# An attention and MLP kernel: a second output product made of seven small ones, with q's exps and row sums moved

## The chip, the cores and the metric

The kernel runs on one core of a Trainium2 chip. The metric is the device time of one execution in microseconds. The runs of the kernel before gave 255.63, 255.73 and 256.14 us; the median, 255.73, is the time before. The engines are named as in the profile: PE (matrix multiplications), PEld (PE's weight loads), DVE (VectorE), ACT (ScalarE), POOL (GpSimd) and SP (SyncE, here only an issuer of DMAs).

## The reference

Linear attention over 8 batches and 8 heads, 576 tokens of 64 values, and then a two-layer network with an exact GELU on the 4608 rows of 512 values:

```python
q_s = exp(q - max(q, axis=-1));  q_s = q_s / (sum(q_s, axis=-1) + 1e-09)
k_s = exp(k - max(k, axis=2));   k_s = k_s / (sum(k_s, axis=2) + 1e-09)
kv  = einsum('bhsd,bhse->bhde', k_s, v)
x   = einsum('bhsd,bhde->bhse', q_s, kv)      # (8, 8, 576, 64)
x   = x.transpose(0, 2, 1, 3).reshape(4608, 512)
h   = x @ w_in                                 # (4608, 2048)
g   = 0.5 * h * (1 + erf(h / sqrt(2)))
out = g @ w_out                                # (4608, 512)
```

All inputs and the output are float32. The matrix products run in bfloat16 with float32 sums. The maxima are left out in the kernel, since they cancel in the quotients.

## The kernel before

**Chunks.** The rows are worked in nine chunks. Chunk c, 0 to 7, holds the first 512 tokens of batch c; chunk 8 holds the last 64 tokens of all batches. For each chunk there is a phase for the hidden layer (x times w_in, then GELU into g) and one for the output (g times w_out). Chunks 0 and 1 are written apart; chunks 2 to 8 are the loop at the end (L1186): `h_waves` (L478), then `y_phase` (L770), or `y_last` for chunk 8. The order is the order of the program text: each engine works through its own instructions in that order and waits where it needs another engine's result. SP's DMAs go the same way, in one queue, but SP has little else to wait for and so runs far ahead of the text.

**Products by Strassen's scheme in Winograd's form.** Both layers multiply 2 x 2 blocks with seven block products in place of eight. In the output phase the left operand is g, its halves by tokens and by hidden index, and sums of them (tiles s12 and s5, made by `s_parts`, L409, on DVE at the end of the hidden phase); the right operand is w_out's blocks and sums of them, made once. `y_operands` (L682) lists the seven pairs. A product has 256 tokens, 1024 hidden values and 256 output columns: 2 groups of tokens times 8 steps of 128, 16 matmuls of 256 columns. c11, c12, c21 and c22 are the four blocks of the chunk's output, in SBUF.

**Product 3 in seven parts.** From chunk 3 on, product 3 is itself made in this way (class `Two`, from L695): seven small products of four matmuls with 128 columns. Their left operands are quarters of s12's half and four sums of them; POOL makes these sums each chunk (`Two.sums`, L712; four instructions of 128x512 in bfloat16). The sums of the weights were made once (`Two.weights`, L703). Two PSUM banks take the results, "yf" (X, four small blocks) and "yd" (D, one block that collects). `Two.add` (L748) adds them on DVE into c12: the letters a, b and c are adds from D, e and d are adds from X.

**The output phase in order.** PE: product 1, product 5, product 6, small product 1, product 2 (bank "yc"), product 7, small products 6, 5, 2, 4, 3 and 7; then, in `next_x` (L1167), the x matmuls of the next chunk and the kv matmuls of the chunk after that, and product 4. DVE: the copy of c22 (L800), the add for c12, D's adds, `q_sums`, the add of product 2 into c11, the add of product 7 into c22, the copy of one x tile, sums of x for the next hidden phase. ACT: the copy of c11 (L797), the table of Exp, `exp_q` (four instructions) and `exp_k` (one) of the batch two chunks on, the table of GELU, three x tiles, and the copy of c21 after product 4. POOL: a touch of one column that waits for DVE's last sum (`touch_s`, L1163), product 3's four sums, and the eight instructions of `q_scale_parts` (L287). SP: the loads of q, k and v for three chunks on, q's transpose by DMA (`xbar_step`, L345), two stores.

**The hidden phase in order.** PE runs the seven products in waves over eight PSUM banks (`h_waves`, L478), the first two of the four quarters of a half, then the last two. DVE makes sums of x (`x_sums`, L460), adds the e sums (`e_sum`, L526) and r sums (`r_sum`, L529) that give the GELU's inputs, and at the end the sums of g. ACT copies partial results and runs the GELUs. POOL casts v of the batch two chunks on (`cast_v_all`, L192), after a touch of one of the x sums.

**Buffers.** q's, k's inputs have two buffers each, v's input from batch 4 on has one; the other v buffer holds product 3's sums. `roles` (L470) says which PSUM bank has which use, and turns once per chunk.

Of the kernel before, what the change touches and what calls it, by code (L numbers as in the profile page):

```python
# [8 lines left out]
FP32 = mybir.dt.float32  # L9
# [7 lines left out]
def kernel(  # L17
# [87 lines left out]
        for i in range(parts):  # L105
            nc.sync.dma_start(out=f[:, i * n:(i + 1) * n, :], in_=src[:, i * n:(i + 1) * n, :])

    def v_buf(b):

        i = b % 2 if b < 4 else 0  # L110
        return f32in.tile([128, HP, NS * D], FP32, tag=f"vf{i}", name="f", bufs=1)

    def load_pair(b, name, t, parts=1):
        f = v_buf(b) if name == "v" else f32in.tile([128, HP, NS * D], FP32, tag=name + "f")
        st[b][name + "f"] = f
        src = t[b].rearrange("h (p n) d -> (h p) (n d)", n=NS).rearrange("(x q) f -> q x f", q=128)
        n = HP // parts
        for i in range(parts):
            h0 = i * n
            if b == 0 and name == "k" and i == 0:  # L120

                nc.scalar.dma_start(out=f[:, 0, :], in_=src[:, 0, :])
                h0 = 1
            nc.sync.dma_start(out=f[:, h0:(i + 1) * n, :], in_=src[:, h0:(i + 1) * n, :])

    def load_k1(i):

        if i == 0:
            st[1]["kf"] = f32in.tile([128, HP, NS * D], FP32, tag="kf", name="f")
        src = k[1].rearrange("h (p n) d -> (h p) (n d)", n=NS).rearrange("(x q) f -> q x f", q=128)  # L130
        nc.sync.dma_start(out=st[1]["kf"][:, 2 * i:2 * i + 2, :], in_=src[:, 2 * i:2 * i + 2, :])

    def load_v1(i):

        if i == 0:
            st[1]["vf"] = v_buf(1)
        src = v[1].rearrange("h (p n) d -> (h p) (n d)", n=NS)
        nc.sync.dma_start(out=st[1]["vf"][:, i, :], in_=src[i * 128:(i + 1) * 128, :])

    def load(b):  # L140
        load_main(b, "q", q)
        load_pair(b, "k", k)
        load_pair(b, "v", v)

    def load_qrest():
        f = f32in.tile([128, 2048], FP32, tag="qf")
# [325 lines left out]
    def turn_roles():  # L472
# [2 lines left out]
        roles.update(bb=r["bb"], ba=r["kv1"], x0=r["x3"], x1=r["kv0"], x2=r["x0"], x3=r["ba"],  # L475
                     kv0=r["x1"], kv1=r["x2"])

    def h_waves(c, mid):  # L478


# [60 lines left out]
        if mid:  # L541
            seed(1)
            mm(1, 2, 3)
            mm(2, 0, 1)
            gelu("C", 0, 1)
            mm(5, 0, 1)
            p5_copy(0, scopy)
            p5_copy(1, scopy)
            x_sums(c, (3, 4))
            seed(2, vcopy)  # L550
            seed(3, vcopy)
            mm(6, 0, 1)
# [24 lines left out]
            gelu("r", 2, 3)  # L577
            mm(3, 2, 3)
            mm(4, 2, 3)
        else:  # L580
            mm(5, 0, 1)
            seed(1)
            p5_copy(0, scopy)
            p5_copy(1, scopy)
            mm(6, 0, 1)
            x_sums(c, (3,))
            e_sum(0)
            e_sum(1)
            x_sums(c, (4,))
            if c + 2 < B:  # L590
                nc.gpsimd.tensor_copy(out=scr[:, 2:3], in_=t4[:, 0, 0:1])
                cast_v_all(c + 2)
            mm(2, 0, 1)
            gelu("C", 0, 1)
            mm(7, 0, 1)
            r_sum(0)
            r_sum(1)
            mm(3, 0, 1)
            for q in (2, 3):
                mm(5, q)  # L600
                mm(1, q)
            mm(4, 0, 1)
            gelu("r", 0)
            gelu("B", 0, 1)
            gelu("r", 1)
            seed(2)
            seed(3)
            gelu("A", 0, 1)
            p5_copy(2, vcopy)
            p5_copy(3, vcopy)  # L610
            s_parts(c, 0, 4, (1,))
            mm(6, 2, 3)
            e_sum(2)
            e_sum(3)
            s_parts(c, 0, 4, (2,))
            mm(2, 2, 3)
            gelu("C", 2, 3)
            mm(7, 2, 3)
            r_sum(2)
            r_sum(3)  # L620
            gelu("r", 2, 3)
            mm(3, 2, 3)
            mm(4, 2, 3)
# [7 lines left out]
        else:  # L631
            s_parts(c, 0, 4, (3, 4))
            s_parts(c, 4, 4, (1, 2, 3, 4))
        turn_roles()
        if mid:
            roles.update(ba=roles["x2"], x2=roles["ba"])
# [57 lines left out]
    class Two:  # L694
# [8 lines left out]
        def weights(self):  # L703
            (b11, b12), (b21, b22) = self.halves(self.raw_w(), slice(0, 4))
            t1, t2, t3, t4 = (self.w[:, i] for i in range(4))
            for o, i0, i1 in ((t1, b12, b11), (t2, b22, t1), (t3, b22, b12), (t4, b21, t2)):
                tt(o, i0, i1, ALU.subtract, eng=nc.gpsimd)

        def raw_w(self):
            return wo_bf[:, DN, HN:DM]  # L710

        def sums(self, c):  # L712

            (a11, a21), (a12, a22) = self.halves(y_operands(c)[0][self.m], slice(0, 4))
            s1, s2, s3, s4 = (self.s[:, i] for i in range(4))
            tt(s1, a21, a22, eng=nc.gpsimd)
            for o, i0, i1 in ((s2, s1, a11), (s4, a12, s2), (s3, a11, a21)):
                tt(o, i0, i1, ALU.subtract, eng=nc.gpsimd)

        def begin(self, c, X, D):  # L720
            self.A, self.W = y_operands(c)[0][self.m], self.raw_w()
            self.X, self.D = X, D
            self.begun = set()

        def mm(self, *sets):

# [32 lines left out]
                }[i]  # L759
                tt(t, t, x)  # L760

    def two_begin():

        t = f32in.tile([128, 9, 512], BF16, tag="vf1", name="two", bufs=1)
        two[3] = Two(3, *(t[:, i:i + 4].rearrange("p x (i n) -> p x i n", i=4) for i in (0, 4)))
        two[3].weights()

    two = {}

    def y_phase(c, ins):  # L770
# [21 lines left out]
            for fn in ins.get(i, []):  # L792
                fn()

        t3 = two[3] if c > 2 else None
        mm(1, pa, True)
        (nc.vector.tensor_copy if c == 1 else nc.scalar.copy)(out=c11, in_=halves(pa))  # L797
        after(1)
# [1 line left out]
        nc.vector.tensor_copy(out=c22, in_=halves(pb))  # L800
        after(5)
        mm(6, pa, False)
        if t3:
            tt(c12, halves(pa), c22)
            t3.begin(c, bank(at["yb"], "yf"), bank(roles["kv1"], "yd"))
            t3.mm(1)
            t3.add("a", c12)
        else:
            tt(halves(pb), halves(pa), c22)
        after(6)  # L810
        mm(2, pc, True)
        tt(c11, c11, halves(pc))
        after(2)
        mm(7, pa, False)
        if t3:
            t3.mm(6, 5, 2, 4, 3)
            t3.add("b", c12)
            t3.mm(7)
            if c + 2 < B:
                t3.add("c", c12)  # L820
        tt(c22, halves(pa), c22)
        if t3 and c + 2 >= B:
            t3.add("c", c12)
        after(7)
        if not t3:
            mm(3, pb, False)
            nc.scalar.copy(out=c12, in_=halves(pb))
            y_store(c, 0, ysb[0])
            after(3)
        else:  # L830
            ins[3][0](lambda: t3.add("ed", c12))
            y_store(c, 0, ysb[0])
        mm(4, pa, False)
        nc.scalar.copy(out=c21, in_=halves(pa))
        y_store(c, 1, ysb[1])
        after(4)

    def y_last(c):

# [293 lines left out]
    for m in (3, 2, 4, 1):  # L1133
# [11 lines left out]

    y_phase(1, {
        1: [sums[3], lambda: norm_q(2, 0, 2)],
        6: [lambda: norm_q(2, 1, 2, nc.vector), lambda: cast_v_all(3), two_begin, lambda: xbar_step(2), lambda: exp_q(3)],
        2: [lambda: kv_step(2), lambda: exp_k(3)],
        7: [lambda: q_sums(3)],  # L1150
        3: [lambda: table(AF.Gelu)],
        4: [lambda: load(4), lambda: x_all(2, (3, 4, 1, 5)),
            lambda: kv_step(3, lambda: x_sums(2, (1,))), lambda: x_sums(2, (2,))],
    })

    def q_late():


        nc.gpsimd.tensor_copy(out=scr[:, 2:3], in_=quad["r"][:, 0, 0, 0:1])
        q_scale(3, nc.gpsimd)  # L1160
        xbar_step(3)

    def touch_s():  # L1163

# [18 lines left out]
        if fn:  # L1183
            fn()

    for c in range(2, B + 1):  # L1186
        nb = c + 2
        h_waves(c, q_late if c == 2 else None)
        yi = {}
        if nb <= B:  # L1190
            yi[1] = [lambda: exp_q(nb)]
            yi[6] = [lambda: q_sums(nb), lambda: q_scale_parts(nb)]
            yi[7] = [lambda: table(AF.Gelu)]
        if nb + 1 < B:
            yi[6].append(lambda: load(nb + 1))
        elif nb + 1 == B:
            yi[6].append(load_qrest)
        if nb < B:
            yi[5] = [lambda: exp_k(nb), touch_s]
            if c == 2:  # L1200
                yi[5].append(lambda: cast_v_all(nb))
        if 2 < c < B:
            yi.setdefault(5, []).append(lambda: two[3].sums(c))
        if c < B:
            yi[3] = [lambda *fn: next_x(c, nb, *fn)]
            y_phase(c, yi)
        else:
            y_last(c)


# [28 lines left out]
```

## Time and profile before

| what | value |
|---|---|
| median of the runs | 255.73 us |
| profiled execution | 255.67 us |
| its span, first to last instruction | 253.9 us |
| granted TensorE clock, mean | 0.999 |
| busy time in 98.6 to 124.3 (about chunk 3's period): PE, DVE, ACT, POOL | 25.70, 20.34, 21.50, 11.68 us of 25.70 |
| the same in 124.3 to 150.0 | 25.70, 21.01, 21.85, 12.29 us of 25.70 |
| the same in 200.7 to 225.7 (about chunk 7's) | 25.00, 18.64, 14.08, 6.02 us of 25.00 |

A line of the timeline gives the start in microseconds from the span's start, the length, the engine, the line of the program, the operation, what it writes and reads with shapes, how many instructions were merged into it, and in brackets the idle time of the engine before it and what ended it. Matmuls are pipelined: the distance between two starts is what a group costs PE, and the length of the last one reaches some 0.16 us into the next. PEld is PE's weight loads; they run ahead of the matmuls by about 0.1 us.

### The profile page before, as it was taken

What the parts mean: (1) busy time and instruction counts of PE and PEld (TensorE: products, weight loads), DVE (VectorE), ACT (ScalarE), POOL (GpSimd) and SP (SyncE); (2) the same over time, 40 slices, a digit from 0 to 9 for tenths busy, and PEclk for the clock granted to TensorE, in tenths of its full rate; (3) what the DMA queues carried; (4) which work ended last, traced back from release to release, by engine and by line L of the source; (5) the groups of instructions that cost most, each with busy time, mean ns of one, the idle gap of its engine ahead of it and who ended that gap; (6) DMA issues with size and microseconds to landing.
All of it is one profiled execution on the core that took longest, in us unless ns stands there. A gap on an engine that the chain in (4) does not pass through costs nothing.

```text
span 253.9 us, 6709 instructions
## 1 busy us (share of the span) xinstructions
PE 247.0 (97%) x2738; PEld 195.9 (77%) x2738; DVE 195.9 (77%) x352; ACT 191.4 (75%) x334; POOL 82.6 (33%) x112
## 2 busy tenths in 40 slices
PE   7799999999999999999999999999999999999994
PEld 3444445448888888889888988898888888998883
DVE  1878699877987986898789877987788889478932
ACT  4785988699887986899788968896887687068810
POOL 1530023000945065408640774077007700700000
PEclk9999999999999999999999999999999999999999
DMA  7999999994289998980199109400700070012033
GB/s 235 400 397 427 399 407 399 398 413 172 56 260 371 239 375 259 314 332 1 34 293 403 63 20 296 102 0 6 250 0 3 0 250 0 3 67 101 1 83 85
DMA packets 43166, 50.23 MB, mean 198 GB/s; under 512 B 20224, under 2 KB 30464, under 8 KB 42880
## 3 DMA queue, kind: packets, MB, share of 16 engines
q1 hardware_dynamic: 42416, 49.13, 56.3%
q10 hardware_dynamic: 720, 0.69, 1.0%
q8 instruction: 21, 0.34, 0.5%
q14 instruction: 9, 0.07, 0.1%
HBM read 36.70 MB, written 9.44 MB: 182 GB/s over the span
## 4 chain that ended last, share of the span: by engine, by line
PE 93%; DMA 4%; ACT 0%; ACTq 0%; issue 0%; DVE 0%; POOL 0%
PE ya L785 20%; PE qa L512 19%; PE ps L401 11%; PE qb L512 10%; PE yb L785 6%; PE ps L658 6%; PE qc L512 5%; PE yc L785 5%; PE ya L857 2%; DMA touch<-in_moe_w_in_dram 2%; DMA f<-in_v_dram 2%; PE kv L225 2%; PE yf L743 2%; PE ps L367 2%; PE yb L857 1%; PE yd L743 1%
## 5 line engine op out<-in xcount | busy, mean ns | idle before, releaser
L512 PEld LDWEIGHTS <-quad_s 128*128 128x128 bf16 x448 | 43.8, 98 | 5.3
L785 PEld LDWEIGHTS <-g 128*128 128x128 bf16 x448 | 43.0, 98 | 5.9 <-issue 0.4
L512 PEld LDWEIGHTS <-wi_bf 128*128 128x128 bf16 x336 | 32.9, 98 | 4.0 <-issue 0.2
L512 PE MATMUL qa<-quad_t,quad_s 128*128 128x256 bf16 x224 | 29.4, 272 | 0.0
L401 PE MATMUL ps<-xT,wi_bf 128*128 128x512 bf16 x128 | 28.1, 379 | 0.0
L785 PEld LDWEIGHTS <-s 128*128 128x128 bf16 x256 | 25.0, 98 | 2.9
L785 PE MATMUL ya<-w,g 128*128 128x256 bf16 x224 | 26.8, 273 | 0.0
L444 DVE TENSOR_TENSOR qb<-qa,r 128x512 f32<-128x512 f32 x28 | 18.2, 694 | 11.0 <-ACT r L524 4.5
L292 POOL TENSOR_TENSOR e<-e,recq 128x256 bf16<-128x256 bf16 x40 | 24.7, 655 | 4.0 <-issue 2.1
L283 POOL TENSOR_TENSOR e<-e,recq 128x1024 bf16<-128x1024 bf16 (+1 forms) x4 | 9.3, 2332 | 48.5 <-DVE recq L278 41.8
L394 ACT CAST xT<-ps 128x512 bf16<-128x512 f32 x23 | 12.3, 593 | 16.7 <-PE ps L372 8.4
L277 DVE TENSOR_REDUCE qsum<-e 128x16 f32<-128x1024 bf16 (+1 forms) x12 | 20.9, 1741 | 4.7 <-ACT e L173 4.6
L401 PEld LDWEIGHTS <-wi_bf 128*128 128x128 bf16 x128 | 12.4, 98 | 15.1 <-issue 0.5
L407 ACT ACTIVATE g<-ps 128x512 bf16<-128x512 f32 x32 | 17.6, 602 | 6.1 <-PE ps L401 5.8
L536 ACT ACTIVATE g<-r 128x512 bf16<-128x512 f32 x28 | 17.3, 631 | 6.2 <-DVE r L444 6.2
L173 ACT ACTIVATE e<-f 128x512 bf16<-128x512 f32 (+1 forms) x42 | 20.5, 556 | 2.0 <-DMA f<-in_q_dram 1.8
L444 POOL TENSOR_TENSOR two<-s 128x512 bf16<-128x512 bf16 x10 | 11.6, 1156 | 29.8 <-DVE s L444 29.8
L536 ACT ACTIVATE g<-qc 128x512 bf16<-128x512 f32 x28 | 15.2, 594 | 6.4 <-PE qc L512 6.4
L444 DVE TENSOR_TENSOR r<-qa,r 128x512 f32<-128x512 f32 x28 | 18.0, 683 | 0.8 <-PE qa L512 0.7
L190 POOL CAST v_aug<-f 128x576 bf16<-128x576 f32 x25 | 17.3, 732 | 2.7 <-DMA f<-in_v_dram 2.6
L178 ACT ACTIVATE ek<-f 128x2304 bf16<-128x2304 f32 (+1 forms) x10 | 17.2, 1726 | 0.5 <-DMA f<-in_k_dram 0.5
L785 PE MATMUL yb<-wo_bf,s 128*128 128x256 bf16 x144 | 17.2, 273 | 0.0
(114 smaller groups left out, 492.8 us busy)
## 6 DMA issues: line engine op xcount, KB each, us to landing
out_dram<-y_sb SPq DMA_DIRECT2D x16, 512.0 KB, 3.8
f<-in_k_dram SPq DMA_DIRECT2D x6, 1152.0 KB, 10.1
f<-in_v_dram SPq DMA_DIRECT2D x6, 1152.0 KB, 11.1
f<-in_q_dram SPq DMA_DIRECT2D x6, 1024.0 KB, 7.6
w<-in_moe_w_in_dram SPq DMA_DIRECT2D x6, 512.0 KB, 8.9
f<-in_v_dram SPq DMA_DIRECT2D x8, 288.0 KB, 6.2
f<-in_q_dram SPq DMA_DIRECT2D x4, 512.0 KB, 9.0
w<-in_moe_w_out_dram SPq DMA_DIRECT2D x2, 1024.0 KB, 11.9
```

What stands on the lines that cost most here:

```text
L173: nc.scalar.activation(out=dst[:, i], in_=src[:, u], func=AF.Exp)
L178: nc.scalar.activation(out=ek[b % 2][:, i:i + n], in_=st[b]["kf"][:, i:i + n].rearrange("p x (n d) -> p x n d", n=NS), func=AF.Exp,)
L190: eng.tensor_copy(out=o, in_=i)
L277: nc.vector.reduce_sum(out=qsum, in_=st[b]["eq"][:, :, i * w:(i + 1) * w, :], axis=AX.X)
L292: nc.gpsimd.tensor_tensor(out=e, in0=e, op=ALU.mult, in1=st[b]["recq"][:, j, i:i + 4].unsqueeze(2).to_broadcast([128, 4, D]),)
L401: nc.tensor.matmul(ps, wi_bf[:, dm, t * 128:(t + 1) * 128], st[c]["xT"][:, dm, :], start=(dm == 0), stop=(dm == NDM - 1),)
L407: nc.scalar.activation(out=st[c]["g"][:, t, :], in_=ps, func=AF.Gelu)
L444: eng.tensor_tensor(out=out, in0=in0, in1=in1, op=op)
L512: nc.tensor.matmul(held[kind, q][:, u], w, mov[m][:, k], start=(m in (1, 5) and u == 0 and k == 0), stop=(k == 1), skip_group_check=True,)
L536: nc.scalar.activation(out=g[:, t:t + 2, half], in_=held[kind, q], func=AF.Gelu)
L658: nc.tensor.matmul(ps, st[c]["g"][:, t, j * 128:(j + 1) * 128], wo_bf[:, t, :], start=(t == 0), stop=(t == NDF - 1),)
L785: nc.tensor.matmul(ps[:, j * HN:(j + 1) * HN], act[m][:, k, j * 128:(j + 1) * 128], wgt[m][:, k, :], start=(first and k == 0 and j == 0), ...
```

## The change

- Product 2 is made of seven small products too, in chunks 3 to 7, by a second `Two`. Its weights' sums are made once on POOL (three instructions in chunk 2's hidden phase, one in its output phase). The four sums of its left operand are made on DVE, after `s_parts`. Its results go to half of the bank of D and to the bank "ye"; the adds into c11 are on DVE.
- A new function, `y_inner`, has the output phase of chunks 3 to 7, with another order of the products: 1, 5, 6, small 1 of product 3, small 1, 5, 2 and 4 of product 2, half of 7, small 6 of 2, the other half of 7, small 6 of 3, small 7 and 3 of 2, small 5, 2, 4 and 7 of 3, small 3 of 3, then `next_x` and product 4. The copy of c22 goes from DVE to ACT. POOL's touch reads the last of product 2's sums. The four sums of product 3 are made in another order.
- `exp_q` runs one chunk earlier, behind `exp_k`; chunk 2 runs it for two batches. q's row sums go into the hidden phase of the next chunk, in two halves (`q_part`); the reciprocals stay in the output phase (`q_rest`).
- Loads are issued behind these exps, k and v for three chunks on, q for four (`load_late`). k has two buffers up to batch 3 and one after; the other holds product 2's sums.

```diff
+    def load_late(b):
+        if b < B:
+            load_pair(b, "k", k)
+            load_pair(b, "v", v)
+        if b + 1 < B:
+            load_main(b + 1, "q", q)
+        elif b + 1 == B:
+            load_qrest()
...
+    def q_part(b, i):
+        if i == 0:
+            st[b]["qsum"] = small.tile([128, J, H], FP32, tag="qsum", name="qsum")
+        js = slice(2 * i, 2 * i + 2)
+        nc.vector.reduce_sum(out=st[b]["qsum"][:, js], in_=st[b]["eq"][:, js], axis=AX.X)
...
             x_sums(c, (3,))
+            if c + 2 <= B:
+                q_part(c + 2, 0)
             e_sum(0)
...
             r_sum(1)
+            if c + 2 <= B:
+                q_part(c + 2, 1)
             mm(3, 0, 1)
...
             s_parts(c, 4, 4, (1, 2, 3, 4))
+            if c < B:
+                two[2].sums(c, nc.vector)
...
-            tt(s1, a21, a22, eng=nc.gpsimd)
-            for o, i0, i1 in ((s2, s1, a11), (s4, a12, s2), (s3, a11, a21)):
-                tt(o, i0, i1, ALU.subtract, eng=nc.gpsimd)
+            tt(s1, a21, a22, eng=eng)
+            for o, i0, i1 in ((s2, s1, a11), (s3, a11, a21), (s4, a12, s2)):
+                tt(o, i0, i1, ALU.subtract, eng=eng)
...
+    def y_inner(c, nb):
...
+        mm(1, pa, True)
+        nc.scalar.copy(out=c11, in_=halves(pa))
+        if nb < B:
+            table(AF.Exp)
+        mm(5, pb, True)
+        nc.scalar.copy(out=c22, in_=halves(pb))
+        if nb < B:
+            exp_k(nb)
+            exp_q(nb + 1)
+            load_late(nb + 1)
+        nc.gpsimd.tensor_copy(out=scr[:, 2:3], in_=t2.s[:, 3, 0, 0:1])
+        t3.sums(c, nc.gpsimd)
+        mm(6, pa, False)
+        tt(c12, halves(pa), c22)
+        d = bank(roles["kv0"], "yd")
+        t3.begin(c, bank(roles["bb"], "yf"), d[:, 0:256])
+        t2.begin(c, bank(roles["kv1"], "ye"), d[:, 256:512], ("D",))
+        t3.mm(1)
+        t2.mm(1, 5, 2, 4)
+        t3.add("a", c12)
+        t2.add("a", c11)
+        if nb <= B:
+            q_rest(nb)
+        mm(7, pa, False, (0,))
+        t2.mm(6)
+        t2.add("bd", c11)
+        mm(7, pa, False, (1,))
+        if nb >= B:
+            tt(c22, halves(pa), c22)
+        t3.mm(6)
+        t3.add("b", c12)
+        t2.mm(7, 3)
+        t2.add("ce", c11)
+        t3.mm(5, 2, 4, 7)
+        t3.add("c", c12)
+        t3.mm(3)
+        if nb < B:
+            tt(c22, halves(pa), c22)
+            table(AF.Gelu)
+        if nb <= B:
+            q_scale_parts(nb)
+        next_x(c, nb, lambda: t3.add("ed", c12))
+        y_store(c, 0, ysb[0])
+        mm(4, pa, False)
+        nc.scalar.copy(out=c21, in_=halves(pa))
+        y_store(c, 1, ysb[1])
...
-        4: [lambda: load(4), lambda: x_all(2, (3, 4, 1, 5)),
+        4: [lambda: load(4), lambda: load_main(5, "q", q), lambda: x_all(2, (3, 4, 1, 5)),
...
+        late.extend(two_begin(2, "kf1"))
+        for fn in late[0:3]:
+            fn()
+
+    h_waves(2, q_late)
+    y_phase(2, {
+        1: [lambda: exp_q(4)],
+        5: [lambda: exp_k(4), touch_s, lambda: cast_v_all(4), late[3]],
+        6: [lambda: q_sums(4), lambda: q_scale_parts(4), lambda: load_late(5), lambda: exp_q(5)],
+        7: [lambda: table(AF.Gelu)],
+        3: [lambda: next_x(2, 4)],
+    })
+    for c in range(3, B + 1):
+        h_waves(c, None)
+        if c < B:
+            y_inner(c, c + 2)
+        else:
+            y_last(c)
```

More of the change, by code (lines that the diff above doesn't have):

```diff
@@ L106, in load_main, with kv_buf @@
             nc.sync.dma_start(out=f[:, i * n:(i + 1) * n, :], in_=src[:, i * n:(i + 1) * n, :])
-    def v_buf(b):
+    def kv_buf(b, name):
         i = b % 2 if b < 4 else 0
-        return f32in.tile([128, HP, NS * D], FP32, tag=f"vf{i}", name="f", bufs=1)
+        return f32in.tile([128, HP, NS * D], FP32, tag=f"{name}f{i}", name="f", bufs=1)
     def load_pair(b, name, t, parts=1):
-        f = v_buf(b) if name == "v" else f32in.tile([128, HP, NS * D], FP32, tag=name + "f")
+        f = kv_buf(b, name)
         st[b][name + "f"] = f
@@ L128, in load_k1 @@
         if i == 0:
-            st[1]["kf"] = f32in.tile([128, HP, NS * D], FP32, tag="kf", name="f")
+            st[1]["kf"] = kv_buf(1, "k")
         src = k[1].rearrange("h (p n) d -> (h p) (n d)", n=NS).rearrange("(x q) f -> q x f", q=128)
@@ L135, in load_v1 @@
         if i == 0:
-            st[1]["vf"] = v_buf(1)
+            st[1]["vf"] = kv_buf(1, "v")
         src = v[1].rearrange("h (p n) d -> (h p) (n d)", n=NS)
@@ L476, in turn_roles, with q_rest @@
                      kv0=r["x1"], kv1=r["x2"])
+    def q_part(b, i):
[3 more added lines that the diff above has]
+        nc.vector.reduce_sum(out=st[b]["qsum"][:, js], in_=st[b]["eq"][:, js], axis=AX.X)
+    def q_rest(b):
+        st[b]["recq"] = small.tile([128, J, H], FP32, tag="recq", name="recq")
+        nc.vector.reciprocal(st[b]["recq"], st[b]["qsum"])
     def h_waves(c, mid):
@@ L706, in weights, with sums, begin @@
             for o, i0, i1 in ((t1, b12, b11), (t2, b22, t1), (t3, b22, b12), (t4, b21, t2)):
-                tt(o, i0, i1, ALU.subtract, eng=nc.gpsimd)
+                yield lambda o=o, i0=i0, i1=i1: tt(o, i0, i1, ALU.subtract, eng=nc.gpsimd)
         def raw_w(self):
-            return wo_bf[:, DN, HN:DM]
-        def sums(self, c):
+            return wo_bf[:, DN, (HN if self.m == 3 else 0):][:, :, 0:HN]
+        def sums(self, c, eng):
             (a11, a21), (a12, a22) = self.halves(y_operands(c)[0][self.m], slice(0, 4))
             s1, s2, s3, s4 = (self.s[:, i] for i in range(4))
-            tt(s1, a21, a22, eng=nc.gpsimd)
-            for o, i0, i1 in ((s2, s1, a11), (s4, a12, s2), (s3, a11, a21)):
-                tt(o, i0, i1, ALU.subtract, eng=nc.gpsimd)
-        def begin(self, c, X, D):
+            tt(s1, a21, a22, eng=eng)
+            for o, i0, i1 in ((s2, s1, a11), (s3, a11, a21), (s4, a12, s2)):
+                tt(o, i0, i1, ALU.subtract, eng=eng)
+        def begin(self, c, X, D, begun=()):
             self.A, self.W = y_operands(c)[0][self.m], self.raw_w()
             self.X, self.D = X, D
-            self.begun = set()
+            self.begun = set(begun)
         def mm(self, *sets):
@@ L760, in add, with two_begin @@
                 tt(t, t, x)
[L762 to L766, printed above, removed]
+    def two_begin(m, tag):
+        t = f32in.tile([128, 9, 512], BF16, tag=tag, name="two", bufs=1)
+        two[m] = Two(m, *(t[:, i:i + 4].rearrange("p x (i n) -> p x i n", i=4) for i in (0, 4)))
+        return list(two[m].weights())
     two = {}
@@ L793, in after @@
                 fn()
-        t3 = two[3] if c > 2 else None
         mm(1, pa, True)
@@ L802, in y_phase @@
         mm(6, pa, False)
[L803 to L809, printed above, removed]
+        tt(halves(pb), halves(pa), c22)
         after(6)
@@ L814, in y_phase @@
         mm(7, pa, False)
[L815 to L820, printed above, removed]
         tt(c22, halves(pa), c22)
-        if t3 and c + 2 >= B:
-            t3.add("c", c12)
         after(7)
[L825 to L832, printed above, removed]
+        mm(3, pb, False)
+        nc.scalar.copy(out=c12, in_=halves(pb))
+        y_store(c, 0, ysb[0])
+        after(3)
         mm(4, pa, False)
@@ L836, in y_phase, with halves, mm @@
         after(4)
+    def y_inner(c, nb):
+        act, wgt = y_operands(c)
+        pa, pb = (bank(roles[n], "y" + n) for n in ("ba", "bb"))
+        ysb = [moe_sb.tile([128, 2, DM], FP32, tag="y_sb", name="y_sb", bufs=2) for i in range(2)]
+        c11, c12 = ysb[0][:, :, 0:HN], ysb[0][:, :, HN:DM]
+        c21, c22 = ysb[1][:, :, 0:HN], ysb[1][:, :, HN:DM]
+        t2, t3 = two[2], two[3]
+        def halves(ps):
+            return ps.rearrange("p (j n) -> p j n", j=2)
+        def mm(m, ps, first, js=(0, 1)):
+            for j in js:
+                for k in range(HK):
+                    nc.tensor.matmul(
+                        ps[:, j * HN:(j + 1) * HN], act[m][:, k, j * 128:(j + 1) * 128],
+                        wgt[m][:, k, :], start=(first and k == 0 and j == 0),
+                        stop=(k == HK - 1), skip_group_check=True,
+                    )
+        mm(1, pa, True)
[40 more added lines that the diff above has]
+        next_x(c, nb, lambda: t3.add("ed", c12))
+        y_store(c, 0, ysb[0])
+        mm(4, pa, False)
+        nc.scalar.copy(out=c21, in_=halves(pa))
+        y_store(c, 1, ysb[1])
     def y_last(c):
@@ L1147 @@
         1: [sums[3], lambda: norm_q(2, 0, 2)],
-        6: [lambda: norm_q(2, 1, 2, nc.vector), lambda: cast_v_all(3), two_begin, lambda: xbar_step(2), lambda: exp_q(3)],
+        6: [lambda: norm_q(2, 1, 2, nc.vector), lambda: cast_v_all(3), lambda: [f() for f in two_begin(3, "vf1")], lambda: xbar_step(2), lambda: exp_q(3)],
         2: [lambda: kv_step(2), lambda: exp_k(3)],
@@ L1151 @@
         3: [lambda: table(AF.Gelu)],
-        4: [lambda: load(4), lambda: x_all(2, (3, 4, 1, 5)),
+        4: [lambda: load(4), lambda: load_main(5, "q", q), lambda: x_all(2, (3, 4, 1, 5)),
             lambda: kv_step(3, lambda: x_sums(2, (1,))), lambda: x_sums(2, (2,))],
     })
[L1156 to L1161, printed above, removed]
     def touch_s():
@@ L1184, in next_x, with q_late @@
             fn()
[L1186 to L1203, printed above, removed]
+    late = []
+    def q_late():
+        nc.gpsimd.tensor_copy(out=scr[:, 2:3], in_=quad["r"][:, 0, 0, 0:1])
+        q_scale(3, nc.gpsimd)
+        xbar_step(3)
+        late.extend(two_begin(2, "kf1"))
[11 more added lines that the diff above has]
+        h_waves(c, None)
         if c < B:
-            yi[3] = [lambda *fn: next_x(c, nb, *fn)]
-            y_phase(c, yi)
+            y_inner(c, c + 2)
         else:
```

## The prediction

> **What bounds the kernel now.** I read the page first: the shares of busy time, then the chain that ended last.
>
> ```profile
> PE 247.0 (97%) x2738; PEld 195.9 (77%) x2738; DVE 195.9 (77%) x352; ACT 191.4 (75%) x334; POOL 82.6 (33%) x112
> PE 93%; DMA 4%; ACT 0%; ACTq 0%; issue 0%; DVE 0%; POOL 0%
> ```
>
> PE bounds it; in chunks 3 to 7 nothing but PE stands on the chain. So the change is worth what it takes from PE's instruction stream, less every new wait that it puts into that stream. Next, the timeline of chunk 4 on PE from the start of its output products, 136.42, which I call zero (times after it are written +x):
>
> ```profile
> 136.42 1.91 PE L785 MATMUL ya<-wo_bf,g 128*128 128x256 bf16 x16
> 141.66 0.39 PE L743 MATMUL yd<-wo_bf,s 128*128 128x128 bf16 x4
> 141.88 1.91 PE L785 MATMUL yc<-wo_bf,g 128*128 128x256 bf16 x16
> 143.63 1.91 PE L785 MATMUL ya<-w,g 128*128 128x256 bf16 x16
> 145.38 0.39 PE L743 MATMUL yd<-two 128*128 128x128 bf16 x4
> 146.49 0.39 PE L743 MATMUL yd<-two 128*128 128x128 bf16 x4
> 146.81 0.63 PE L367 MATMUL ps<-qT,kvc 64*64 64x512 bf16 x8
> ```
>
> By distances of starts, a full product of 16 matmuls takes 143.63 - 141.88 = 1.75 us, and one small product of four takes (146.49 - 145.38) / 5 = 0.222 us. No gaps: PE has no slack here. The same stretch on POOL and DVE shows who prepares the sums that the small products of product 3 read:
>
> ```profile
> 139.44 0.69 DVE L444 TENSOR_TENSOR s<-g,s 128x1024 bf16<-128x1024 bf16 x1
> 140.26 0.19 POOL L1165 CAST scr<-s 128x1 f32<-128x1 bf16 x1 [9.18 <-DVE s L444]
> 140.40 1.16 POOL L444 TENSOR_TENSOR two<-s 128x512 bf16<-128x512 bf16 x1
> 141.64 1.15 POOL L444 TENSOR_TENSOR two<-two,s 128x512 bf16<-128x512 bf16 x1
> 142.87 1.16 POOL L444 TENSOR_TENSOR two<-s,two 128x512 bf16<-128x512 bf16 x1
> 143.99 1.16 POOL L444 TENSOR_TENSOR two<-s 128x512 bf16<-128x512 bf16 x1
> ```
>
> DVE ends its sums at +3.71; POOL, which waited for that, starts 0.13 later and has its last sum at +8.73. PE wants the first of them at +8.96. That is a margin of 0.23 us behind a chain DVE, POOL, PE.
>
> **The change, part by part.** Chunks 3 to 7, five times each unless said.
>
> *Product 2 in seven parts (PE).* 7 x 0.222 = 1.55 in place of 1.75: -0.19 per chunk, -0.96 in all. These are rows of the same shape (product 3 runs so already), so little can be wrong. Against it speaks the Trainium skill, "TensorE: Matmul & The Clock Gate", section Back-to-back issue gap: it gives about 81 ns a matmul of 128 columns in a stream with weight loads. By that figure the product would take an estimated 28 x 81 ns = 2.27 us, +0.52 per chunk. The trace disagrees: 0.222 / 4 = 55.5 ns, in every chunk from 3 to 7.
>
> *Product 2's four input sums (DVE), put after the last of the sums at the end of the hidden layer.* Nearest row, 128x512 bf16 sums with POOL quiet, four in the same order of dependence, in chunk 1:
>
> ```profile
> 48.85 0.42 DVE L444 TENSOR_TENSOR s<-g 128x512 bf16<-128x512 bf16 x1 [0.49 <-ACT g L407]
> 49.31 0.43 DVE L444 TENSOR_TENSOR s<-s,g 128x512 bf16<-128x512 bf16 x1
> 49.66 0.42 DVE L444 TENSOR_TENSOR g<-g 128x512 bf16<-128x512 bf16 x1
> 49.99 0.42 DVE L444 TENSOR_TENSOR s<-g,s 128x512 bf16<-128x512 bf16 x1
> ```
>
> 49.99 + 0.42 - 48.85 = 1.56 us. DVE starts the first at +3.62 (0.60 after the op at 139.44, the usual distance) and ends the last at +5.18. DVE itself loses nothing: the copy of c22 that stood there (681 ns) goes to ACT, and its next work, c12, waits for PE until +5.50 anyway.
>
> *POOL's wait.* Its touch instruction now reads the last of these four sums, not the last of the old ones. Queued behind it on POOL are product 3's four sums, then the eight scalings of q; PE waits for the sums. Touch at +5.18 + 0.13 = +5.31, first sum at +5.45, four sums in 4.64 (distances 1.24, 1.12, 1.12 and 1.16 for the last, now the one that small product 3 reads) to 4.75 (as in the fence): the last ends at +10.09 to +10.20. From POOL to PE's weight load 0.06 us pass:
>
> ```profile
> 8.04 1.90 POOL L283 TENSOR_TENSOR e<-e,recq 128x1024 bf16<-128x1024 bf16 x1 [6.74 <-ACT e L173]
> 10.00 0.45 PEld L311 LDWEIGHTS <-e 128*128 128x128 bf16 x8 [1.70 <-POOL e L283]
> ```
>
> So the load could go at +10.15 to +10.26. When does PE want it? Before small product 3 of product 3 come three full products and product 7 (5.24 + 1.75) and 13 small ones (13 x 0.222 = 2.89): +9.87, its weight load 0.11 before, +9.76. PE stalls 0.39 to 0.50 per chunk; I take 0.44, 2.2 in all. Ends: sums at the closest distance (0.33) and POOL at 1.12 throughout bring the load to +9.87, a stall of 0.1; chunk 3's touch, which came at +4.19 instead of +3.84 for a reason the trace does not show, gives 0.9. The other sums are in time: small product 6 loads at +8.2 and its sum is there at +7.9; product 7's at +9.0 for +9.5.
>
> *Adds into c11 (DVE).* Before, one add of 643 ns; now 283, 283, 287, 422 and 675 = 1.95. With the sums (+1.56), the copy gone (-0.68) and the row sums in two (2 x 1.206 - 2.277 = +0.13), DVE gains 1.95 - 0.64 + 1.56 - 0.68 + 0.13 = 2.3 us on 20.7 to 21.0 busy of 25.7. On the path: the last read of product 3's small bank ends at about +10.5, before the kv matmuls want that bank (+10.6, and +11.1 with the stall). Today that handover is late: kv takes 0.82 to 0.86 here and 0.76 in chunk 1 where nothing is in its way. With PE stalled just before, this goes: -0.2 over the three chunks that have it.
>
> *c22's copy on ACT, q's exps a chunk ahead.* ACT gets one copy of 0.59. c11 copied at +2.5, table 1.28, copy, exp_k 2.1, exps 2.2, table and its touch 1.5: free at +10.2; the first x copy is wanted at +10.6 to +11.1. Hidden, with 0.4 left; if that goes, the next hidden layer starts late by the excess. In chunk 2 both sets of exps run: ACT is free 2.1 us later (96.55 for 94.45) where x was ready at 96.05, so x comes 1.0 later, at 98.1, and the next layer starts at 98.47: 0 to +0.3, I take 0.05.
>
> *q's row sums in the hidden layer (DVE).* The first half (1.21) goes into the idle 1.03 to 1.69 before the e sums, the second into 0.47 + 0.18 + 0.51 = 1.16 after the r sums. Cover nearly exact; and DVE reaches the first gap earlier, since PE stalled and the 2.28 + 0.35 of row sums left the output phase. PE lost 0.03, 0.08 and 0.07 to the e sums in chunks 4 to 6 (0.90, 0.95, 0.94 for 0.873); I take half back, -0.1. Ends -0.2 and +0.15 x 4 = +0.6, for DVE is in a chain with PE there; +0.1 for the second half.
>
> *Loads (SP).* k, v and the next q are now issued behind exp_k, since k has one buffer: about +6.6, 15 us later than today (101.47 to 105.33 for chunk 6's). k and v land in 10 to 11 us, about +18; POOL's casts want v at +17.8 and have until its next touch, 13 us on; exp_k wants k at +30. Behind them on SP wait the transpose, which POOL's scaling releases at about +15.7 (+14.3 today), and the two stores, landing at about +22, wanted by the next copies at +27.6. Hidden. Product 2's weight sums, four of 1.16 on POOL, once, lie in its idle 8.8 us of chunk 2. Costs nothing.
>
> Sum against the profiled execution, 255.67 (span 253.9 and 1.8 around it; the median of the runs, 255.73, is 0.06 above): -0.96 + 2.2 - 0.2 - 0.1 + 0.1 + 0.05 = +1.1. **256.8 us**, 0.4% slower.
>
> **The rivals.**
> *The handover is in time (the other side).* If product 3's last sum reached PE by +9.7, nothing would be left of the stall, and the time were 255.67 - 0.96 - 0.3 = 254.4. For it: the sums were put in exactly the order of use, with this one last; POOL needs to be just half a microsecond faster than worked out. Against it: every distance in the chain is a row. It decides at a stall of 0.1 per chunk: under that the kernel is faster by over 0.2%.
> *Half of it.* Stalls of 0.15 to 0.3 cancel the gain: about 255.7.
> *DVE becomes the bound.* At 23 of 25.7 us in one strict order, a delay of one add reaches kv and product 4. 0.25 more per chunk on top of the stall: 258.0. For it: between c12 and c22 stand five more adds, with 0.1 to 0.2 to spare at the kv bank. Against: DVE waits for PE at +5.50 today, and gaps remain.
> *Small products slow down.* Eight sets of four stand in a row now, six today. If each matmul there had to wait for its own weight load, 98 ns in the rows of weight loads, 28 would take 2.74 us, +1.0 per chunk for -0.19, with PE too late to meet the stall: 260.4. Against it: 55.5 ns a matmul all through today's six sets in a row. 1%. (The page named above stands between: by its 81 ns this case would come to an estimated 258.)
>
> **How the numbers follow.** A run of this kernel tells about 0.2% (0.5 us) from no change. Stall as worked out (0.3 to 0.6): 47%, 256.3 to 257.4. DVE bound: 10%. Slow small products: 1%. Half: 18%. In time: 24%. So slower 0.58, same 0.18, faster 0.24. The range is to hold 8 in 10: it reaches down to 254.5, nearly through the in-time case, and up to 257.9, short of the stalls of 0.9.
>
> **What would show it.** Right: in chunks 4 to 7 PE's weight load before the last small product of product 3 waits for POOL, 0.4 us, and POOL's touch stands at about +5.3; product 2's small products at 0.222; kv at 0.76; the period of a chunk about 25.9 for 25.7. Wrong: no wait on POOL in PE's rows and a period of 25.4; or waits of PE for DVE at the e sums or the kv banks. My sum fails most easily in the 0.44, a difference of two chains of ten microseconds.

## The result, and the profile after

The changed kernel takes **258.49 us** (258.3 to 258.74 in four runs) where the kernel before takes 255.70; the ratio is 1.0106, with a 95% interval from 1.0088 to 1.0123. It is slower, as forecast, but by 2.8 us and not by 1.1, and outside the range given, which ended at 257.9. That the direction came out right was luck, as the part on the prediction shows.

The changed kernel's page: shares of busy time, and the chain that ended last.

```profile
PE 247.5 (96%) x2798; PEld 197.1 (77%) x2798; DVE 206.0 (80%) x391; ACT 191.4 (75%) x339; POOL 86.9 (34%) x118
PE 92%; DMA 4%; DVE 1%; POOL 1%; issue 0%; ACT 0%; SPq 0%; ACTq 0%
```

DVE and POOL now have a share of the chain that they did not have before. The waits in chunks 3 to 7 on PE's two rows of that kernel (who waited for whom: us in total, times, longest):

```profile
PEld L771 <- issue: 3.3, 5, 0.9
PE yd L771 <- DVE y_sb L454: 2.6, 5, 0.8
```

There are five waits, one per chunk, and PE waits for DVE, not for POOL. (The view counts idle time, from the end that it models for the matmuls before; by distances of starts, as below, each wait costs some 0.17 us more.) Line 771 is the small products, `yd` the bank of D. Their place is in the timeline of chunk 4's output phase, which begins at 137.12 here. PE:

```profile
145.44 0.39 PE L771 MATMUL yd<-two 128*128 128x128 bf16 x4
146.21 0.38 PE L771 MATMUL yd<-two 128*128 128x128 bf16 x4 [0.38 <-DVE y_sb L454]
146.43 0.39 PE L771 MATMUL ye<-wo_bf,two 128*128 128x128 bf16 x4
...
147.32 0.39 PE L771 MATMUL yd<-two 128*128 128x128 bf16 x4
147.55 0.39 PE L771 MATMUL yf<-wo_bf,two 128*128 128x128 bf16 x4
```

and DVE, then POOL, in the same stretch:

```profile
144.77 0.29 DVE L454 TENSOR_TENSOR y_sb<-y_sb,yd 128x128 f32<-128x128 f32 x1 [0.61 <-PE yd L771]
...
145.87 0.29 DVE L454 TENSOR_TENSOR y_sb<-y_sb,yd 128x128 f32<-128x128 f32 x1 [0.48 <-PE yd L771]
```

```profile
142.43 0.19 POOL L878 CAST scr<-two 128x1 f32<-128x1 bf16 x1 [10.69 <-DVE two L454]
...
146.02 1.15 POOL L454 TENSOR_TENSOR two<-s,two 128x512 bf16<-128x512 bf16 x1
```

The group at 145.44 is small product 6 of product 3, that at 146.21 small product 7 of product 2. Without a wait the second would stand 0.222 later, at 145.66; it stands 0.55 after that. DVE read product 2's own D long before (144.77 to 145.06). What ends at 145.87 + 0.29 = 146.16, just before PE goes on, is the read of product 3's D, which itself waits for product 6. The two D's are halves of one bank, and product 7 waits for the read of the other half: a round trip PE, DVE, PE in which PE has nothing else to do.

POOL's touch stands at +5.31 and its last sum ends at +10.05, nearly as the prediction had them (+5.31, +10.09 to +10.20). But small product 3 of product 3 now comes at +10.43, since PE lost 0.55 before: POOL is in time, and its lateness does not show.

In chunks 6 and 7 the wait is longer. Chunk 6, PE and DVE:

```profile
198.56 0.38 PE L771 MATMUL yd<-two 128*128 128x128 bf16 x4 [0.75 <-DVE y_sb L454]
```

```profile
197.62 0.69 DVE L454 TENSOR_TENSOR y_sb<-yba,y_sb 128x512 f32<-128x512 f32 x1 [0.27 <-PE yba L862]
198.23 0.28 DVE L454 TENSOR_TENSOR y_sb<-y_sb,yd 128x128 f32<-128x128 f32 x1
```

There DVE does the add into c22 (0.69) before it reads product 3's D. Product 6 stands at 197.41, so product 7 is 198.56 - 197.41 - 0.22 = 0.93 late. In all the bank costs 3 x 0.55 + 2 x 0.93 = 3.5 us.

To compare kernels without the landing of the first loads, I take PE's time from the start of chunk 3's hidden phase (first matmuls of line 512 or 534) to the start of chunk 8's output. It is 139.37 us before and 141.61 in the changed kernel, 2.24 more. Of the 2.8 between the medians the rest lies outside this stretch; the last two runs come back to it.

### The profile page after: what moved, and what is told of

The parts are those of the page before. It is cut to its first block, busy times and chain, and to the rows that moved or that the text cites. A ratio compares the mean times of both kernels' runs of the same rounds, so it can differ in the third digit from the quotient of the medians.

```text
span 256.6 us, 6873 instructions
## 1 busy us (share of the span) xinstructions
PE 247.5 (96%) x2798; PEld 197.1 (77%) x2798; DVE 206.0 (80%) x391; ACT 191.4 (75%) x339; POOL 86.9 (34%) x118
## 4 chain that ended last, share of the span: by engine, by line
PE 92%; DMA 4%; DVE 1%; POOL 1%; issue 0%; ACT 0%; SPq 0%; ACTq 0%
PE qa L534 19%; PE yba L862 14%; PE ps L411 11%; PE qb L534 10%; PE ya L813 6%; PE ps L686 5%; PE qc L534 5%; PE ybb L862 3%; PE yd L771 3%; PE yb L813 3%; PE ya L934 2%; DMA f<-in_v_dram 2%; PE kv L235 2%; PE yf L771 2%; PE ye L771 2%; DMA f<-in_q_dram 2%
## 5 line engine op out<-in xcount | busy, mean ns | idle before, releaser
L862 PEld LDWEIGHTS <-g 128*128 128x128 bf16 x240 | 22.6, 98 | 3.0 <-issue 0.4
L878 POOL CAST scr<-two 128x1 f32<-128x1 bf16 x5 | 0.9, 187 | 64.3 <-DVE two L454 64.3
L862 PE MATMUL yba<-w,g 128*128 128x256 bf16 x160 | 20.0, 273 | 0.0
L862 PEld LDWEIGHTS <-s 128*128 128x128 bf16 x160 | 15.6, 98 | 1.8
L454 DVE TENSOR_TENSOR y_sb<-y_sb,yd 128x128 f32<-128x128 f32 (+1 forms) x32 | 10.1, 327 | 7.8 <-PE yd L771 7.2
```

The lines of the kernel that those rows point to most:

```text
L454: eng.tensor_tensor(out=out, in0=in0, in1=in1, op=op)
L862: nc.tensor.matmul(ps[:, j * HN:(j + 1) * HN], act[m][:, k, j * 128:(j + 1) * 128], wgt[m][:, k, :], start=(first and k == 0 and j == 0), ...
```

## The experiments

Each edit is against the changed kernel. The ratios are to the kernel before, run on the same chip; "stretch" is the PE time just defined.

### A bank of its own for product 2's D

```diff
-        t2.begin(c, bank(roles["kv1"], "ye"), d[:, 256:512], ("D",))
+        t2.begin(c, bank(roles["kv1"], "ye"), bank(roles["x0"], "yd2"))
```

> Product 2's D gets a PSUM bank of its own (that of x0, free in this phase). Shared-bank theory (small product 7 of product 2 waits until DVE has read product 3's D, since both lie in one bank): the 0.55 us before that product in chunks 3 to 5 and 0.93 in chunks 6 and 7 go, 3.5 in all; then product 3's last sum on POOL, which is ready at +10.05, stalls small product 3 of product 3 by about 0.35 per chunk, 1.75 in all: 256.7. Handover theory of the prediction (POOL alone): no change, 258.5. A third, that DVE has too much to do: the stall stays with another cause, 258 to 258.5.

Measured: 255.92 us, ratio 0.9997 (0.9988 to 1.0007), stretch 139.10. PE's only wait left on another engine in chunks 3 to 7, and chunk 4 on PE and POOL (its output begins at 136.56):

```profile
PEld L771 <- POOL two L454: 1.0, 5, 0.2
```

```profile
146.22 0.39 PE L771 MATMUL yd<-two 128*128 128x128 bf16 x4
146.67 0.40 PE L771 MATMUL yf<-wo_bf,two 128*128 128x128 bf16 x4
```

```profile
145.46 1.15 POOL L454 TENSOR_TENSOR two<-s,two 128x512 bf16<-128x512 bf16 x1
```

The wait on DVE is gone in all five chunks; DVE had time for its adds. Behind it stands the wait that the prediction named: POOL ends at 146.61, +10.05, and the last small product goes 0.06 later, at +10.11 for the +9.88 that its place gives. It costs 0.23 to 0.25 in chunks 3 to 5 and 0.15 in chunks 6 and 7, 1.0 in all, not the 0.35 per chunk expected or the prediction's 0.44. The prediction had set the weight load 0.11 ahead of the matmul and the handover before it; here the whole way from POOL's end to the matmul is 0.06.

### POOL started earlier, banks still shared

```diff
-        nc.gpsimd.tensor_copy(out=scr[:, 2:3], in_=t2.s[:, 3, 0, 0:1])
+        nc.gpsimd.tensor_copy(out=scr[:, 2:3], in_=s12[:, HK - 1, HT:HT + 1])
```

> POOL's touch reads the last of the old sums as before the change, so POOL starts product 3's sums 1.4 us earlier; the banks stay shared. Shared-bank theory: no gain, since the PE wait on DVE comes first and hides POOL's lateness; DVE's four sums run against POOL's and take longer (0.65 to 0.8 where 0.42), so 258.5 to 259.5. Handover theory: -2.2, 256.3.

Measured: 272.81 us, ratio 1.065 (1.0628 to 1.0673), 14.3 us above the changed kernel and far outside both expectations. Chunk 4 (output from 140.70) on DVE, POOL and PE:

```profile
144.32 0.42 DVE L454 TENSOR_TENSOR two<-g 128x512 bf16<-128x512 bf16 x1
144.78 1.40 DVE L454 TENSOR_TENSOR two<-two,g 128x512 bf16<-128x512 bf16 x1
146.10 1.37 DVE L454 TENSOR_TENSOR two<-g 128x512 bf16<-128x512 bf16 x1
147.40 1.37 DVE L454 TENSOR_TENSOR two<-g,two 128x512 bf16<-128x512 bf16 x1
```

```profile
145.98 1.22 POOL L454 TENSOR_TENSOR two<-two,s 128x512 bf16<-128x512 bf16 x1
147.16 1.33 POOL L454 TENSOR_TENSOR two<-s 128x512 bf16<-128x512 bf16 x1
```

```profile
149.42 1.03 PE L862 MATMUL yba<-w,g 128*128 128x256 bf16 x8 [2.20 <-DVE y_sb L454]
```

DVE's first sum, before POOL starts, takes 0.42; the three beside POOL's take 1.4 each, one per POOL instruction. DVE reaches c12 at 148.69, +7.99 in place of +5.49, and PE stands 2.36 us before the first half of product 7 (146.84 + 0.22 to 149.42), whose bank the c12 add still reads. The same pause, 2.36 or 2.37, stands in all five chunks, 11.8 in all. Chunk 4 loses nothing else (its period is 28.28 for 26.03), nor do 6 and 7. Chunks 3 and 5 lose 3.75 each: after their pause the granted clock falls, in chunk 3 to 0.82 in 119 to 122 and 0.61 in 122 to 125, in chunk 5 to 0.68 in 177.7 to 183, where chunk 4 keeps 1.00, and small products stand up to 0.43 apart. The mean clock is 0.987 in all four runs of this kernel, so this belongs to it; why only two of the five pauses are followed by a lower clock, no run shows. The mechanism of the pause was in the expectation, its price was not: I had taken 0.65 to 0.82 from the x sums that run beside POOL's scaling of q. The Trainium skill, "SBUF — State Buffer", section Who interferes with whom, says that a DVE instruction with two SBUF inputs contends with a GpSimd instruction that reads SBUF, and calls the ports that the two share an exclusive lock. The trace agrees: 1.37 for 0.42 beside a POOL operation of 1.15 to 1.33.

### Product 7 of product 2 ahead of product 6 of product 3

```diff
-        t3.mm(6)
-        t3.add("b", c12)
-        t2.mm(7, 3)
+        t2.mm(7)
+        t3.mm(6)
+        t3.add("b", c12)
+        t2.mm(3)
```

> Banks shared as in the change, but small product 7 of product 2 goes before small product 6 of product 3, and its other neighbours stay. Shared-bank theory: product 7 then has to wait only for a read that ended half a microsecond before; the first stall goes, except for 0.1 to 0.3 where small product 7 of product 3 now waits for two reads of the bank, and POOL's 0.35 shows: 256.7 to 257.6, most gained in chunks 6 and 7. If DVE is simply too late with everything: 258.5.

Measured: 255.93 us, ratio 0.9998 (0.9988 to 1.0009), stretch 139.11: the own bank's result with the bank still shared. The two products now follow each other without a gap and product 3's D is read after both. PE in chunk 4:

```profile
145.14 0.61 PE L771 MATMUL yd<-two 128*128 128x128 bf16 x8
```

In chunks 3 to 5 POOL's 0.23 to 0.24 is all that is left. The small wait expected at small product 7 of product 3 came in chunks 6 and 7 alone, 0.14 and 0.13, and took the place of POOL's there. PE in chunk 6, where DVE ends its reads of the bank at 197.82:

```profile
197.52 0.39 PE L771 MATMUL yf<-two,s 128*128 128x128 bf16 x4
197.88 0.38 PE L771 MATMUL yd<-two 128*128 128x128 bf16 x4
```

So not the amount of work on DVE made PE wait, but the order of writes and reads in one bank.

### c22 after the D's in chunks 6 and 7

```diff
-        if nb >= B:
-            tt(c22, halves(pa), c22)
         t3.mm(6)
...
-        if nb < B:
-            tt(c22, halves(pa), c22)
+        tt(c22, halves(pa), c22)
```

> In chunks 6 and 7 DVE adds product 7 into c22 after product 3's D, as chunks 3 to 5 do, not before. Shared-bank theory: the wait in chunks 6 and 7 falls from 0.93 to 0.55, -0.75 in all: 257.7. Handover theory: 258.5.

Measured: 258.54 us, ratio 1.0097 (1.0079 to 1.0114), stretch 141.62: no gain. The wait at product 7 did fall to 0.55 (197.62 to 198.38 in chunk 6), but the time came back at product 4, which needs the bank that c22 is read from. PE in chunk 6:

```profile
201.00 1.91 PE L862 MATMUL yba<-w,g 128*128 128x256 bf16 x16 [0.34 <-DVE y_sb L454]
```

Product 4 starts 0.41 us later behind the x matmuls than in the changed kernel (0.97 for 0.56), about the 0.38 gained before: one wait took another's place.

### The last small product behind the kv matmuls

On top of the own bank, small product 3 of product 3 goes from in front of `next_x` to behind its kv matmuls (in chunks 6 and 7, which have none, behind the x matmuls).

```diff
-        t3.mm(3)
...
-        next_x(c, nb, lambda: t3.add("ed", c12))
+        next_x(c, nb, lambda: t3.add("ed", c12), lambda: t3.mm(3))
```

> Own bank for product 2's D, and small product 3 of product 3, which waited 0.23 us per chunk for POOL's last sum (146.67 for 146.44 with the own bank alone), moved behind the kv matmuls of the chunk after next. Nested-waits theory (first the shared bank, behind it POOL): the 0.23 go in five chunks, -1.15: 254.8, and below the kernel before by 0.4%. If the gain of the small products is eaten by something else, such as DVE's adds reaching kv or product 4: 255.5 to 256.

Measured: 255.11 us, ratio 0.9962 (0.9949 to 0.9976), stretch 138.28. The wait on POOL is gone. 0.82 is gained where 1.15 was expected; that counted 0.23 in all five chunks, and the waits were 1.0 together. A part of the rest goes to pauses at the changed places: in chunk 4 the kv matmuls start 0.58 after the x matmuls where 0.46 is usual.

### One of POOL's sums on DVE

On top of the own bank; POOL makes sums 1, 2 and 4 of product 3.

```diff
-                two[2].sums(c, nc.vector)
+                two[2].sums(c, nc.vector, (1, 2))
+                two[3].sums(c, nc.vector, (3,))
+                two[2].sums(c, nc.vector, (3, 4))
...
-        t3.sums(c, nc.gpsimd)
+        t3.sums(c, nc.gpsimd, (1, 2, 4))
```

> Own bank, and one of POOL's four sums (the third) made on DVE between product 2's, so that POOL starts 0.34 later but has three sums in place of four and ends at about +9.4 for +10.05. Nested-waits theory: PE no longer waits for POOL, 254.8; small product 6 of product 3 wants POOL's second sum at +8.25 and could lose up to 0.1 per chunk, 255.3. If the wait on POOL is not what is left: 255.9.

Measured: 254.77 us, ratio 0.9951 (0.9939 to 0.9963), stretch 138.05. PE has no wait for DVE or POOL in chunks 3 to 7. This is faster than both kernels, by 0.5% against the kernel before.

### POOL's touch on the third sum

On top of the own bank:

```diff
-        nc.gpsimd.tensor_copy(out=scr[:, 2:3], in_=t2.s[:, 3, 0, 0:1])
+        nc.gpsimd.tensor_copy(out=scr[:, 2:3], in_=t2.s[:, 2, 0, 0:1])
```

> Own bank for product 2's D, and POOL's touch reads the third of DVE's four sums, not the fourth: POOL starts 0.34 earlier. DVE's fourth sum has begun by then (third ends at +4.84, POOL's first sum starts at about +5.1, DVE's fourth runs from +4.76 to +5.18), so they hardly meet. Nested-waits theory: POOL's last sum is ready at +9.7 for PE's +9.88, the 0.23 of waiting per chunk go: 254.8, like the kernel with one sum on DVE. If the two engines do meet there as in the early touch (1.37 for 0.42 us): DVE is 0.6 late at c12, PE waits for product 2's first read of D: 256 to 257.

Measured: 254.92 us, ratio 0.9964 (0.995 to 0.9978), stretch 138.05, the same as the last. Chunk 4's last two small products on PE follow each other with the usual distance:

```profile
145.98 0.39 PE L771 MATMUL yd<-two 128*128 128x128 bf16 x4
146.21 0.39 PE L771 MATMUL yf<-wo_bf,two 128*128 128x128 bf16 x4
```

DVE's fourth sum kept its 0.42 us: it ended at 141.48, and POOL's first sum started at 141.49, so the two did not meet. So POOL can start one sum earlier for nothing; four sums earlier, with the banks still shared, cost 14 us.

### Product 2 whole, the other edits kept

```diff
-        nc.gpsimd.tensor_copy(out=scr[:, 2:3], in_=t2.s[:, 3, 0, 0:1])
+        nc.gpsimd.tensor_copy(out=scr[:, 2:3], in_=s12[:, HK - 1, HT:HT + 1])
...
-        t2.begin(c, bank(roles["kv1"], "ye"), d[:, 256:512], ("D",))
+        pc = bank(roles["x0"], "yc")
...
-        t2.mm(1, 5, 2, 4)
+        mm(2, pc, True)
...
-        t2.mm(6)
-        t2.add("bd", c11)
+        tt(c11, c11, halves(pc))
...
-        t2.mm(7, 3)
-        t2.add("ce", c11)
```

The sums on DVE go too.

> Product 2 stays one full product (in the bank of before, one add into c11); all other edits of the change stay: exps and loads, row sums in the hidden phase, c22 on ACT, the halves of product 7, POOL's touch as before. It prices these edits by themselves. Theory that they cost nothing and give back the small waits at kv and at the e sums: 255.4 to 255.7. If they carry part of the change's loss: above 256.2.

Measured: 256.19 us, ratio 1.0003 (0.9993 to 1.0013), stretch 139.45, so no gain, above what was expected. In chunk 6 small product 7 of product 3 waits 0.25 us (197.82 for 197.57), because DVE does c22 before it reads D there; in chunk 7 it waits as long (223.00 for 222.75). Twice 0.25 takes back what the other edits gained: without it the stretch would be 138.95, 0.4 under that of before. So they cost nothing by themselves, but with product 2 whole the place of c22 in the last two chunks does.

### q's row sums back in the output phase

On top of the own bank; both calls of `q_part` go.

```diff
-            q_rest(nb)
+            q_sums(nb)
```

> Own bank, but q's row sums back in the output phase, whole (2.28 us on DVE where the reciprocal stands now); exps stay a chunk ahead. Theory that DVE's time in the output phase is what the move bought: c11's and c12's adds come 2 us late, product 2's small product 7 and the kv bank wait about 1 to 1.5 us in each of chunks 3 to 6: 260 to 262. If DVE had room for them: 256.

Measured: 259.25 us, ratio 1.0124 (1.011 to 1.0138), stretch 142.64, 3.5 above the own bank alone, 0.9 per chunk that has row sums. PE's wait itself is 1.1 in each of these chunks, at the low end of the 1 to 1.5 expected (147.08 for 146.07, and 0.1 more at the product behind it), but the wait on POOL is hidden behind it and no longer paid. The 2.28 of the row sums cost only half of themselves: the gaps in which DVE waits for PE there (0.61 and 0.48 in the changed kernel) take up a part. Chunk 4 on DVE and PE:

```profile
144.22 2.28 DVE L287 TENSOR_REDUCE qsum<-e 128x32 f32<-128x2048 bf16 x1
```

```profile
147.08 0.38 PE L767 MATMUL yd<-two 128*128 128x128 bf16 x4 [0.84 <-DVE y_sb L454]
```

The same small product 7 waits, now for its own D, read behind the row sums. By these numbers (138.05 and 3.5 are more than 139.37) the split of product 2 would not pay without this move; that is worked out, not run.

### Both kernels once more

> The kernel before once more, for the spread of its start: in its first profile the hidden layer of chunk 3 begins on PE at 98.47, in the changed kernel and seven variants at 98.64 to 99.35, though nothing that the change touches is on PE's chain up to there. If the start is chance (the landing of the first loads), this run lies anywhere in 98.4 to 99.4; if the change delays it, at 98.47 again within 0.1.

> The changed kernel once more, for the same. Chance: chunk 3's hidden layer begins anywhere in 98.4 to 99.4 (98.91 in its first profile), and from there to the last chunk's output PE takes 141.6 as in its first profile. 258.5 in all.

Measured: 255.87 us for the kernel before, its chunk 3 begins at 98.67 (98.47 in its first profile), stretch 139.38 (139.37); 258.71 for the changed one, at 98.68 (98.91), stretch 141.54 (141.61). The start is chance by some tenths; the difference between the kernels, 2.2 in the stretch, is not. Both pairs of profiles are some 2.8 apart in all. In the first pair the other half microsecond stands before chunk 3 (0.44), in the second at the end of the span: behind the stretch come 16.05 us before and 16.58 after, where the first pair has 16.06 and 16.08. Whether the change has a part in that half microsecond is not shown.

## Why the prediction was right and wrong

**The sum closes.** With no wait left the stretch is 138.05, 1.32 less than before. Five times 0.19 from the small products makes 0.96 of it; the rest, 0.36, is about what the prediction gave for the waits at kv (0.2; the kv matmuls take 0.79, 0.74 and 0.74 in that kernel for 0.86, 0.83 and 0.82) and at the e sums (0.1, with 0.2 as its end; the five hidden phases are 0.18 shorter). Add the bank's 3.5 and the result is 141.55; 141.61 and 141.54 were measured. For the own bank alone 138.05 + 1.02 (POOL's five waits) = 139.07; measured 139.10.

**The step that failed** is *Adds into c11 (DVE)*. It counted DVE's time and named one handover on the path, the kv bank; for PE waiting on these adds within the output phase the sum has no term. Measured, that is 3.5 us: 0.55 in each of chunks 3 to 5 and 0.93 in each of 6 and 7. The prediction left out that each small product that accumulates in D is a write into a bank that DVE reads in between, and that the two D's share one bank: small product 7 of product 2 stands behind product 3's read too. The diff shows it in one line, `d[:, 256:512]`. "The other sums are in time" was right of POOL's sums and silent on this. The Trainium skill has the rule, in "PSUM — Partial Sum Buffer", section PSUM bank collisions raise a hardware error: two engines must not use one bank (in the same quadrant of partitions) at once, at different addresses neither, so waits are to be set by bank. The trace agrees as far as it can: PE waited for a read of other columns of its bank. Taking the wait away without moving the data was not tried, so no run here shows whether the chip needs it or only the program asks for it.

**POOL's handover** was right as a mechanism and hidden in the changed kernel. Its chain was worked out to 0.1 us, but PE's side was not: PE came 0.55 later than the sum assumed, so of the 2.2 us priced for it none was paid. Where it does come to light, it is 0.15 to 0.25 per chunk and not 0.44. That is why the direction was luck: without the 2.2 the prediction's own sum gives -1.1, a faster kernel, and what made it slower is not in the sum. (By the sum's terms a stall of 0.3 to 0.6 gives 256.1 to 257.6, a little wider than the 256.3 to 257.4 that the prediction states; nothing hangs on it.)

**The price of a small product** was right: the seven sets behind the wait stand 0.223 apart (146.21 to 147.55), and with the wait gone the eight stand 0.224 apart (144.64 to 146.21 with POOL's touch on the third sum), 56 ns a matmul. The figure of about 81 ns that the prediction quoted from the Trainium skill's page "TensorE: Matmul & The Clock Gate" is not borne out here either.

**The rivals.** DVE as the bound, 258.0, came nearest in time, and its place, "between c12 and c22", was right; its reason was not, since with another bank the same adds on the same DVE do not hold PE up. The rival on the other side, 254.4, is what the mended versions come near to: 254.8 and 254.9.

**What cost nothing, as said:** the late loads, exps a chunk ahead, and the copy on ACT: with one of POOL's sums on DVE no wait on them is left on PE, and the stretch closes without a term for them. The row sums fit into the gaps of the hidden phase: the e sums hardly hold PE up any more (0.88 in chunk 4, 0.873 being the time without a wait). The touch at +5.3 and the adds came as announced.

## What to carry to other kernels

Before splitting one product into small ones, list for each PSUM bank the order of writes by PE and reads by DVE: each read between two writes is a round trip (here 0.43 from the matmul's start to DVE, 0.29 for the add, 0.05 back), and it needs other work on PE in between, whichever half of the bank it reads. A wait found in one trace can hide the next behind it: after the first was taken away, 0.15 to 0.25 us per chunk on POOL appeared, and both had to go before the change as a whole paid 0.4 to 0.5%. And a queue's start may be advanced only as far as the engine beside it allows: POOL one sum earlier did not meet DVE's sums and cost nothing, four sums earlier it met three of them.

## What the runs showed of the hardware that I had not expected

Sums of 128x512 bfloat16 on DVE take 0.42 us alone and 1.37 to 1.40 beside the like sums on POOL, which themselves slow from 1.15 to 1.22 to 1.33. Each of the three sums on DVE ends 0.27 to 0.28 after one on POOL, as if the two engines took turns. Three such meetings in each of five chunks made pauses of 11.8 us on PE, most of 14; two of the pauses were followed by a granted clock of 0.6 to 0.8 for some microseconds, which took most of the rest. Beside POOL's scaling of q, DVE's sums of x of the same size took 0.65 to 0.82 before, which is no guide to that.
